# An attention backward kernel on one core: the scores S stay in the crossbar's key order in PSUM, and the exp reorders them

## The chip, the cores and the metric

The kernel runs on one core of a Trainium2 chip. The metric is the device time of one execution in microseconds; the time of a kernel is the median of several runs. A profile is one execution, taken by the hardware profiler.

In the text PE is TensorE (PEld its weight loads), DVE is VectorE, ACT is ScalarE, POOL is GpSimd and SP is SyncE, which here issues most of the transfers.

## The reference

Two independent attention blocks, A and B, each with 8 batches, 96 queries, model width 640, 32 heads of width 128 and a cache of 512 keys. The kernel computes the output and, for a given gradient of the output, the gradients of every input:

```
q      = (x @ wq) per head
scores = q @ k_cache^T * 128**-0.5          # 96 x 512 per batch and head
p      = softmax(scores)
o      = p @ v_cache
out    = (o of all heads) @ wo
outputs: out, and the gradients of x, k_cache, v_cache, wq, wo
```

So there are 2 x 32 x 8 = 512 pairs of a batch and a head. The text calls each of them a head.

## The kernel before

**Staging.** Heads are taken in pairs (HP = 2) with one batch at a time. A pair loads four tiles: K and V as they lie in memory (p_ldn, L256), and K and V transposed by the DMA crossbar (p_ldT, L242), each 256 KB for two heads. It stores two: dV and dK (p_st, L265). All six are issued by SP, in one queue and in the order of the program. KT_p, VT_p, K_sb and V_sb have four buffers each; dV_sb and dK_sb, the results on their way out, have two. GpSimd's queue issues the weights' loads and the other stores.

**Ticks.** Each head is cut into steps with a tick of their own (OFF): the scores at tick 3, P's transpose and dV at 4, the output at 5, dP and dS at 6, dS's transpose and dK at 7, dQ at 8. One tick takes one step of each of several heads. An Emitter sorts the steps by tick and by a slot within it; the scores, the exp and P are written with a higher priority, and the program's builder orders each engine's instructions from that. Between the heads' steps lie projections, weight gradients and the sums over heads (lines 215, 230, 440, 455, 477 and 512), which the text calls other matmuls.

**The steps of a head.**

- L285, PE: S = QT_h^T x KT into one PSUM bank of 96 x 512 f32.
- L287, DVE: the negated maximum of each row of S.
- L297, ACT: the exp of S, from PSUM to E_sb in bf16, with the row sums.
- L307, DVE: the reciprocal of the sums. L316, POOL: P_sb = E_sb times it.
- L339, PE: P_sb transposed; L345, ACT: copied out. L356, PE: dV; L361, ACT: copied out.
- L332, PE: the output of the head; L342, DVE: copied out. L370, POOL: its product with dO.
- L380, PE: dP = dOT_h^T x VT, also 96 x 512 f32. L382, PE: the row term dl.
- L384, DVE: dS = (dP - dl) * P.
- L406, PE: dS transposed; L408, DVE: copied out. L422, PE: dK; L427, ACT: copied out. L399, PE: dQ; L412, ACT: copied out.

**The order of the keys.** The crossbar's tile has for each of 128 partitions 64 x 16 elements: for each (f, c) 16 neighbouring values, 8 of one head and 8 of the other. Key number is r * 64 + f * 4 + c, with r from 0 to 7, f from 0 to 15 and c from 0 to 3. Everything behind the softmax wants the keys in the order (c, r, f), because K_sb and V_sb are cut into four chunks by c. For K the view is turned into that order when the matmul reads it, so that the innermost walk is over f, 64 elements (128 bytes) apart. For V the matmul reads (f, c, r), with runs of 8 neighbours, so dP lies in PSUM in that order, and L384 turns it with its read pattern: its innermost walk is over f, 32 f32 numbers (128 bytes) apart.

Of the kernel before, what the change touches and what calls it, by code (L numbers as in the profile page):

```python
# [7 lines left out]
ACT = mybir.ActivationFunctionType  # L8
# [48 lines left out]
def build_block(tc, em, tick0, blk, x, kc, vc, wq, wo, g_all, out_all, dx, dk, dv, dwq, dwo, ident, ones, pools, HG=4, first=True, groups=None):  # L57
    nc = tc.nc
# [7 lines left out]
    KC = Sk // 128  # L66
    scale = float(Dh) ** -0.5
# [35 lines left out]
    CS = pools["CS"]  # L103
# [131 lines left out]
    F4 = Sk // R8 // KC  # L235

    def p_ldT(h, b, which):
        def f():
            key = "KT" if which == 0 else "VT"
            t_ = kvp.tile([128, F4 * KC, 16], BF16, name=key + "_p", bufs=4)  # L240
            src = (kc if which == 0 else vc)[b, h:h + HP].rearrange("h (r f) d -> (h r) (f d)", r=R8)
            nc.sync.dma_start_transpose(t_[:], src)  # L242
            for j in range(HP):
                half = t_[:, :, j * R8:(j + 1) * R8]
                if which == 0:
                    CS.setdefault((blk, h + j, b), {})[key] = half.rearrange("p (f c) r -> p c r f", c=KC)
                else:
                    CS.setdefault((blk, h + j, b), {})[key] = half.rearrange("p (f c) r -> p f c r", c=KC)
        return f

    def p_ldn(h, b, which):
# [39 lines left out]
    def c_s2b(h, b):  # L291
        def f():
            with tc.high_priority(PRIO_OFF):
                st = CS[(blk, h, b)]
                E_sb = wk.tile([Sq, Sk], BF16, name="E_sb", bufs=2)
                rowsum = wk.tile([Sq, 1], F32, name="rowsum", bufs=3)
                nc.scalar.activation(E_sb[:], st["S_ps"][:], ACT.Exp, bias=st["negm"][:], scale=1.0, accum_out=rowsum[:])  # L297
                st["E_sb"], st["rowsum"] = E_sb, rowsum
                del st["S_ps"]
        return f  # L300
# [229 lines left out]
    for g in range(NG):  # L530
        h0 = GH0[g]
        for hh in range(groups[g]):
            h = h0 + hh
            j = h % HP
# [170 lines left out]
```

## Time and profile before

| | us |
|---|---|
| median of 3 runs | 2016.59 |
| lowest and highest run | 2014.18, 2019.17 |
| the profiled execution | 2013.47 |
| its span, first to last instruction | 2011.7 |
| DVE busy, ACT busy | 1439.6, 1359.0 |
| POOL busy | 723.5 |

The profile has a page with the shares of each engine, the transfer queues, the chain of work that ended last, and groups of instructions by line. Further views are the timeline, the waits, and a table of windows, with busy time for any stretch of the span. A row of a group gives line, engine, operation, output and input, shapes and count; behind the bar come busy time, the mean of one in ns, and the idle time ahead of it with what ended it. Matmuls overlap on PE, and a duration there holds the time from the first input to the last output, so that the distance between two starts is what an instruction costs the next one.

### The profile page before, as it was taken

Reading aid. Unit: us, or ns where it says so; the run is one execution under the profiler, and the core shown is the slowest. Engines: PE = TensorE matmul, PEld = TensorE weight load, DVE = VectorE, ACT = ScalarE, POOL = GpSimd, SP = SyncE. Lnnn points to the kernel's source line nnn. Section 1 sums busy time; section 2 is a strip of 40 time slices with the busy share of each in tenths; the row PEclk is TensorE's granted clock in tenths of the full one; section 3 lists DMA queues with packets and bytes.
Section 4 is the critical chain, followed back from the end, with each engine's and each line's share of the span. In section 5 each row is a group of like instructions: output and inputs, shape, how many; then the busy total and the mean of one; then the engine's idle time right before and its main releaser. Section 6 shows DMA issues by size and latency. Waiting matters only on the chain.

```text
span 2011.7 us, 59742 instructions
## 1 busy us (share of the span) xinstructions
PE 1957.6 (97%) x22648; PEld 1370.4 (68%) x22648; DVE 1439.6 (72%) x3597; ACT 1359.0 (68%) x3529; POOL 723.5 (36%) x1322
## 2 busy tenths in 40 slices
PE   6999999999999999998999999999999999999998
PEld 4667676676767667666666676767667676676766
DVE  4776777777777777777676767777777777777776
ACT  4877866767666676765666777666676766767663
POOL 3333333333333333334354333333333333333335
PEclk9999999999999999999999999999999999999999
DMA  8998989988889888888889989888898989979883
GB/s 246 257 263 214 251 233 232 251 223 240 228 223 244 230 243 223 235 234 227 213 247 266 253 226 249 226 236 234 232 240 220 238 231 237 252 211 239 229 217 127
DMA packets 322913, 468.88 MB, mean 233 GB/s; under 512 B 37472, under 2 KB 301152, under 8 KB 314432
## 3 DMA queue, kind: packets, MB, share of 16 engines
q1 hardware_dynamic: 304672, 404.75, 77.2%
q0 software_dynamic: 17952, 60.31, 9.1%
q8 instruction: 177, 2.90, 0.6%
q14 instruction: 112, 0.92, 0.1%
HBM read 171.57 MB, written 159.12 MB: 164 GB/s over the span
## 4 chain that ended last, share of the span: by engine, by line
PE 91%; DMA 3%; issue 2%; DVE 2%; POOL 1%; ACT 1%; POOLq 0%; SPq 0%; DVEq 0%; ACTq 0%
PE S_ps L285 21%; PE q_ps L215 10%; PE o_ps L512 9%; PE dV_ps L356 5%; PE dK_ps L422 5%; PE dP_ps L380 5%; PE dwq_ps L477 5%; PE dwo_ps L455 5%; PE dq_dst_ps L406 4%; PE optp_ps L339 4%; PE optp_ps L332 4%; PE dq_dst_ps L399 4%; PE n_ps L230 3%; PE nat_ps L440 2%; DMA out_dram<-ob 1%
## 5 line engine op out<-in xcount | busy, mean ns | idle before, releaser
L297 ACT ACTIVATE E_sb<-S_ps,negm 96x512 bf16<-96x512 f32 x512 | 348.2, 680 | 379.1 <-DVE negm L287 377.0
L287 DVE TENSOR_REDUCE negm<-S_ps 96x1 f32<-96x512 f32 x512 | 351.3, 686 | 257.8 <-PE S_ps L285 256.5
L285 PE MATMUL S_ps<-KT_p,QT_h 128*96 128x512 bf16 x512 | 521.8, 1019 | 2.6 <-DVE ob L523 1.2
L316 POOL TENSOR_SCALAR P_sb<-E_sb,rinv 96x512 bf16<-96x512 bf16 x512 | 352.4, 688 | 417.1 <-DVE rinv L307 414.1
L370 POOL TENSOR_TENSOR prod<-OT_h,dOT_h 128x96 bf16<-128x96 bf16 x512 | 186.7, 365 | 682.6 <-DVE OT_h L342 668.7
L384 DVE SCALAR_TENSOR_TENSOR dS_sb<-dP_ps,dl_ps,P_sb 96x512 bf16<-96x512 f32 x512 | 383.0, 748 | 50.7 <-PE dl_ps L382 37.6
L427 ACT ACTIVATE dK_sb<-dK_ps 128x512 bf16<-128x512 f32 x512 | 301.7, 589 | 159.1 <-PE dK_ps L422 111.2
L361 ACT ACTIVATE dV_sb<-dV_ps 128x512 bf16<-128x512 f32 x512 | 306.5, 599 | 4.4 <-PE dV_ps L356 3.2
L345 ACT ACTIVATE PT_sb<-optp_ps 128x384 bf16<-128x384 bf16 x512 | 251.2, 491 | 0.6 <-PE optp_ps L339 0.5
L356 PE MATMUL dV_ps<-dOnat_h,P_sb 96*128 96x128 bf16 x2048 | 199.6, 220 | 0.0
L422 PE MATMUL dK_ps<-Qnat_h,dS_sb 96*128 96x128 bf16 x2048 | 199.4, 220 | 0.0
L380 PE MATMUL dP_ps<-VT_p,dOT_h 128*96 128x512 bf16 x512 | 196.9, 385 | 0.0
L408 DVE COPY dST_sb<-dq_dst_ps 128x384 bf16<-128x384 bf16 x512 | 177.4, 346 | 23.7 <-PE dq_dst_ps L406 22.9
L406 PE MATMUL dq_dst_ps<-ident,dS_sb 96*128 96x96 bf16 x2048 | 173.2, 207 | 16.4 <-DVE dS_sb L384 16.4
L512 PEld LDWEIGHTS <-OT_h 128*128 128x128 bf16 x1152 | 101.4, 99 | 118.7 <-issue 104.1
L512 PEld LDWEIGHTS <-dQT_h 128*128 128x128 bf16 x1152 | 102.3, 99 | 115.9 <-issue 97.5
L339 PE MATMUL optp_ps<-ident,P_sb 96*128 96x96 bf16 x2048 | 172.8, 206 | 2.9 <-POOL P_sb L316 2.2
L332 PE MATMUL optp_ps<-PT_sb,V_sb 128*128 128x96 bf16 x2048 | 173.4, 207 | 0.0
L399 PE MATMUL dq_dst_ps<-dST_sb,K_sb 128*128 128x96 bf16 x2048 | 171.7, 207 | 0.0
L477 PEld LDWEIGHTS <-x_nat 128*128 128x128 bf16 x1920 | 120.8, 98 | 58.2 <-issue 46.6
L399 PEld LDWEIGHTS <-K_sb 128*128 128x128 bf16 x2048 | 134.2, 98 | 35.2 <-issue 16.7
L512 PE MATMUL o_ps<-wo_r,OT_h 128*128 128x256 bf16 (+1 forms) x1152 | 152.6, 256 | 0.2 <-ACT E_sb L297 0.2
(79 smaller groups left out, 3471.6 us busy)
## 6 DMA issues: line engine op xcount, KB each, us to landing
out_dram<-dV_sb SPq DMA_DIRECT2D x256, 256.0 KB, 3.7
out_dram<-dK_sb SPq DMA_DIRECT2D x256, 256.0 KB, 3.8
V_sb<-in_A_v_cache_dram SPq DMA_DIRECT2D x128, 256.0 KB, 3.9
K_sb<-in_A_k_cache_dram SPq DMA_DIRECT2D x128, 256.0 KB, 3.9
V_sb<-in_B_v_cache_dram SPq DMA_DIRECT2D x128, 256.0 KB, 3.8
K_sb<-in_B_k_cache_dram SPq DMA_DIRECT2D x128, 256.0 KB, 3.9
out_dram<-dwo_sb POOLq DMA_DIRECT2D x64, 160.0 KB, 3.8
out_dram<-dwq_sb POOLq DMA_DIRECT2D x32, 320.0 KB, 6.0
```

The lines of the kernel that those rows point to most:

```text
L285: nc.tensor.matmul(S_ps[:], hs["QT_h"][:, tok], st["KT"], start=True, stop=True)
L287: nc.vector.tensor_reduce(negm[:], S_ps[:], axis=AX.X, op=ALU.max, negate=True)
L297: nc.scalar.activation(E_sb[:], st["S_ps"][:], ACT.Exp, bias=st["negm"][:], scale=1.0, accum_out=rowsum[:])
L316: nc.gpsimd.tensor_scalar(P_sb[:], st["E_sb"][:], st["rinv"][:], 0.0, op0=ALU.mult, op1=ALU.add)
L356: nc.tensor.matmul(dV_ps[:, c * 128:(c + 1) * 128], P_sb[:, c * 128:(c + 1) * 128], hs["dOnat_h"][:, b * 128:(b + 1) * 128], start=True, s ...
L361: nc.scalar.activation(dV_p[:, j], dV_ps[:], ACT.Identity, scale=1.0)
L380: nc.tensor.matmul(dP_ps[:], hs["dOT_h"][:, tok], st["VT"], start=True, stop=True)
L384: nc.vector.scalar_tensor_tensor(dS_sb[:].rearrange("q (a f) -> q a f", f=F4), dP_ps[:].rearrange("q (f a) -> q a f", f=F4), dl_ps[:, 0:1] ...
L399: nc.tensor.matmul(dQT_ps, st["K_sb"][:, c, :], st["dST_sb"][:, c * Sq:(c + 1) * Sq], start=(c == 0), stop=(c == KC - 1))
L422: nc.tensor.matmul(dK_ps[:, c * 128:(c + 1) * 128], dS_sb[:, c * 128:(c + 1) * 128], hs["Qnat_h"][:, b * 128:(b + 1) * 128], start=True, s ...
L427: nc.scalar.activation(dK_p[:, j], dK_ps[:], ACT.Identity, scale=1.0)
L512: nc.tensor.matmul(o_ps[:], src[:, t * 128:(t + 1) * 128], rhs, start=(hh == 0), stop=(hh == groups[g] - 1))
```

## The change

The view of K is now the one of V, so S lies in PSUM in the order (f, c, r). The maximum does not depend on the order. The exp reads S with the pattern that L384 uses for dP, and writes E_sb contiguously in the order (c, r, f), as before.

```
@@ p_ldT
             for j in range(HP):
                 half = t_[:, :, j * R8:(j + 1) * R8]
-                if which == 0:
-                    CS.setdefault((blk, h + j, b), {})[key] = half.rearrange("p (f c) r -> p c r f", c=KC)
-                else:
-                    CS.setdefault((blk, h + j, b), {})[key] = half.rearrange("p (f c) r -> p f c r", c=KC)
+                CS.setdefault((blk, h + j, b), {})[key] = half.rearrange("p (f c) r -> p f c r", c=KC)
@@ c_s2b
-                nc.scalar.activation(E_sb[:], st["S_ps"][:], ACT.Exp, bias=st["negm"][:], scale=1.0, accum_out=rowsum[:])
+                nc.scalar.activation(E_sb[:].rearrange("q (a f) -> q a f", f=F4), st["S_ps"][:].rearrange("q (f a) -> q a f", f=F4), ACT.Exp, bias=st["negm"][:], scale=1.0, accum_out=rowsum[:])
```

F4 is 16, and a stands for the 32 values of (c, r).

## The prediction

> **What bounds the kernel now.** I read the page first: shares, queues, chain, groups.
>
> ```profile
> PE 1957.6 (97%) x22648; PEld 1370.4 (68%) x22648; DVE 1439.6 (72%) x3597; ACT 1359.0 (68%) x3529; POOL 723.5 (36%) x1322
> ...
> DMA packets 322913, 468.88 MB, mean 233 GB/s; under 512 B 37472, under 2 KB 301152, under 8 KB 314432
> ...
> q1 hardware_dynamic: 304672, 404.75, 77.2%
> q0 software_dynamic: 17952, 60.31, 9.1%
> q8 instruction: 177, 2.90, 0.6%
> q14 instruction: 112, 0.92, 0.1%
> ...
> PE 91%; DMA 3%; issue 2%; DVE 2%; POOL 1%; ACT 1%; POOLq 0%; SPq 0%; DVEq 0%; ACTq 0%
> ...
> L297 ACT ACTIVATE E_sb<-S_ps,negm 96x512 bf16<-96x512 f32 x512 | 348.2, 680 | 379.1 <-DVE negm L287 377.0
> L287 DVE TENSOR_REDUCE negm<-S_ps 96x1 f32<-96x512 f32 x512 | 351.3, 686 | 257.8 <-PE S_ps L285 256.5
> L285 PE MATMUL S_ps<-KT_p,QT_h 128*96 128x512 bf16 x512 | 521.8, 1019 | 2.6 <-DVE ob L523 1.2
> ...
> L384 DVE SCALAR_TENSOR_TENSOR dS_sb<-dP_ps,dl_ps,P_sb 96x512 bf16<-96x512 f32 x512 | 383.0, 748 | 50.7 <-PE dl_ps L382 37.6
> ```
>
> PE is busy for 97% of the span of 2011.7 us (the span's own row stands with the windows below) and 91% of the chain, so TensorE is the bound. The costliest thing on it is the S matmul, 512 times 1019 ns. Two other numbers matter later. DVE and ACT are busy about 70% each, off the path. And the DMA rows add up to 77.2 + 9.1 + 0.6 + 0.1 = 87.0% of the sixteen engines' span, or 0.870 x 2011.7 = 1750 us of transfer time. That is more than DVE's, and it is hidden only because PE takes longer.
>
> Next the timeline of one ordinary head (the columns are start, duration, engine, line): TensorE's rows in order, and the one of VectorE that belongs to them.
>
> ```profile
> 1002.17 0.38 PE L380 MATMUL dP_ps<-VT_p,dOT_h 128*96 128x512 bf16 x1
> 1002.39 0.16 PE L382 MATMUL dl_ps<-ones,prod 128*96 128x1 bf16 x1
> 1002.42 0.38 PE L455 MATMUL dwo_ps<-g_nat,Onat 128*128 128x512 bf16 x1
> 1002.63 1.02 PE L285 MATMUL S_ps<-KT_p,QT_h 128*96 128x512 bf16 x1
> 1003.47 1.26 PE L455 MATMUL dwo_ps<-g_nat,Onat 128*128 128x512 bf16 x5
> 1004.57 0.33 PE L399 MATMUL dq_dst_ps<-dST_sb,K_sb 128*128 128x96 bf16 x4
> 1004.74 0.34 PE L406 MATMUL dq_dst_ps<-ident,dS_sb 96*128 96x96 bf16 x4
> ...
> 1002.62 0.75 DVE L384 SCALAR_TENSOR_TENSOR dS_sb<-dP_ps,dl_ps,P_sb 96x512 bf16<-96x512 f32 x1 [0.22 <-PE dl_ps L382]
> ```
>
> The matmul dP has the same shape as S, 128 x 512 with 96 rows out, from a tile that the same transposing load fills. It differs in the order in which it walks that tile. PE starts the instruction behind S after 1003.47 - 1002.63 = 0.84 us, and the one behind dP after 1002.39 - 1002.17 = 0.22 us. Durations overlap on PE, so the distance between starts is the price.
>
> **The change, part by part.** *The S matmul* walks KT_p as dP walks VT_p, in runs of 8 neighbouring elements instead of single elements 128 bytes apart. It should cost what dP costs: 0.84 - 0.22 = 0.62 us less, 512 times, 317 us. All of it lies on PE, the bound. (By the durations it would be 1019 - 380, or 327 us; I take the starts.) From the profiled execution's 2013.47 us, which is its span of 2011.7 and 1.8 around it, this leaves 1696 us if nothing else comes late.
>
> *The maximum* (L287) reads the same 512 numbers of the bank contiguously in another order: nothing.
>
> *The exp* (L297) now reads PSUM with 128 bytes between neighbours and still writes E_sb contiguously. No ACT row shows such a read. The nearest row is L384 on DVE, which reads dP_ps in just this pattern at 748 ns. L287, a contiguous read of the same 96x512 f32, takes 686. So the stride costs at most 62 ns there, though L384 does more besides. From below, nothing suggests a gain, so 0. From above stands what the stride cost PE: 0.62 us. I take the middle of the DVE row, 30 ns, 16 us of ACT time in all, because L384 reads the same memory by the same pattern. ACT then has 1359 + 16 = 1375 us of work, and even with 0.62 us it would have 1359 + 317 = 1676, under the 1696 of PE. On the path it costs nothing while that cover lasts.
>
> The Trainium skill speaks against this part: "PSUM — Partial Sum Buffer", section Specifications (TRN2), gives PSUM lines of 8 bytes and says that a non-contiguous pattern slows matmuls a good deal. Here no matmul has one in PSUM, ACT has; by a penalty of PE's size the sum would still be that of PE. The L384 row speaks against so large a penalty.
>
> No instruction, wait or transfer is added or moved.
>
> *What is late next, among the engines.* PE per head falls from 2011.7 / 512 = 3.93 to 3.31 us; DVE has 1439.6 / 512 = 2.81 and ACT 2.69, so neither is the bound on average. The handoffs tighten. dS ends at 1002.62 + 0.75 = 1003.37, and PE wants it at 1004.74: of 1.37 us of slack 0.75 stays, since one S lies between. It is tighter in a head without other matmuls:
>
> ```profile
> 1965.83 1.02 PE L285 MATMUL S_ps<-KT_p,QT_h 128*96 128x512 bf16 x1
> 1966.67 0.35 PE L399 MATMUL dq_dst_ps<-dST_sb,K_sb 128*128 128x96 bf16 x4
> 1966.90 0.34 PE L406 MATMUL dq_dst_ps<-ident,dS_sb 96*128 96x96 bf16 x4
> ...
> 1969.25 0.35 PE L399 MATMUL dq_dst_ps<-dST_sb,K_sb 128*128 128x96 bf16 x4
> ...
> 1966.09 0.75 DVE L384 SCALAR_TENSOR_TENSOR dS_sb<-dP_ps,dl_ps,P_sb 96x512 bf16<-96x512 f32 x1 [0.27 <-PE dl_ps L382]
> ```
>
> There dS ends at 1966.84, 0.06 us ahead of its use, so such a head loses 0.56 of its 0.62 us again. An estimate: with 3.93 us for a mean head against 1969.25 - 1966.67 = 2.58 for this one (its L399 group to the next one's), most heads have over a microsecond of other matmuls between; I put one head in eight at this loss, 64 x 0.56 = 36 us. So PE alone would give 1696 + 36 = 1732 us.
>
> *What is late next, among the transfers.* The windows view shows how full the DMA engines can be (the last two columns are their busy share and GB/s):
>
> ```profile
> core 0 of [0], span 2011.7 us
> core 0: us, PE busy (x) PEld busy (x) DVE busy (x) ACT busy (x) POOL busy (x), PEclk, DMA share, GB/s
> 0.00:50.00 50.00, 34.70 (x333) 23.19 (x334) 23.12 (x53) 22.04 (x49) 16.57 (x31) 0.97 0.86 246
> 50.00:100.00 50.00, 47.30 (x541) 30.77 (x539) 37.37 (x90) 40.14 (x105) 18.71 (x35) 1.00 1.00 260
> 480.00:520.00 40.00, 39.93 (x473) 27.78 (x471) 30.93 (x79) 29.24 (x78) 15.06 (x29) 1.00 0.99 266
> 1950.00:2011.00 61.00, 52.37 (x650) 40.13 (x647) 40.64 (x105) 27.60 (x72) 33.29 (x62) 0.97 0.47 146
> ```
>
> Where the share is 0.99 to 1.00 the rate is 260 to 266 GB/s. At 1732 us the kernel would ask for 468.88 MB / 1732 us = 271 GB/s on average, its slow start and end included. So the transfers become the bound. First way: 1750 us of transfer time, and the ends, where the engines cannot be full. They idle 0.14 x 50 = 7 us in the first window and 0.53 x 61 = 32 us in the last. 1750 + 39 = 1789. Second way, by bytes: the two ends carry 246 x 50 = 12.3 MB and 146 x 61 = 8.9 MB; the remaining 447.7 MB at 266 GB/s take 1683 us, at 260 GB/s 1722; with the ends' 111 us, shorter by 0.62 us for each of the heads in them (an estimate: six in each, since about half of either window goes to heads of 3.93 us), that is 1683 + 111 - 7 = 1787, or 1826.
>
> **The transfers would come earlier by themselves**, because the queue that issues them waits for PE:
>
> ```profile
> SPq L256 <- PE dK_ps L422: 371.5, 205, 3.4
> ```
>
> These are waits for a buffer that PE is still reading. When PE frees it sooner, the load starts sooner. The one transfer with little room is the store: dV_sb and dK_sb have two buffers, so a store must land within the two heads of the next pair. Where the share was highest, in the window from 50, the chain already ran through it:
>
> ```profile
> 89.04 3.85 DMA out_dram<-dK_sb
> ```
>
> So I expect the loss to show as ACT waiting at L361 and L427 for stores, and PE behind it.
>
> I forecast 1789 us for the span and 1.8 around it: **1790 us**, 224 less than the profiled execution. That one is 0.15% under the median of 2016.59, well inside the range here.
>
> **The rivals.** *The transfers are elastic and PE stays the bound.* The busy share counts the time that packets took, and packets that share an engine or wait for memory count too long; then 1750 us is no floor. The result would be 1732 us, or 1698 if the handoffs cost nothing. For it: no PE wait of weight names a load in steady state, though the share was 0.99 from 480 to 520 with PE busy 39.93 of 40. Against it: the two full windows stop at 260 and 266 GB/s. The Trainium skill is on this side: "DMA: Bandwidth & Descriptors", section Where 436 GB/s comes from, puts the ceiling at 435 GB/s, which would make an estimated 468.88 / 435, or 1078 us. No window here comes near it.
>
> *The stores' landing stops the pair loop before the engines are full.* In the window from 50, PE was busy 47.30 of 50. If that share of its own 1696 + 36 us were all it could hold throughout, the time would be 1732 x 50 / 47.30 = 1831, and where the DMA engines also only reach 0.95, 1750 / 0.95 + 39 = 1881.
>
> *Slower: the exp.* If a 128-byte stride in PSUM costs ACT the ratio that the stride in KT_p costs PE, 0.84 / 0.22 = 3.8, the exp takes 680 x 3.8 = 2584 ns, 1904 more. ACT would have 1359 + 975 = 2334 us and be the bound: 2336 us. This decides from (2011.7 - 1359.0) / 512 = 1.27 us more for each exp on. For it: no ACT row excludes it. Against it: L384.
>
> *No effect.* The matmul's 1.02 us could come from something other than the order of KT_p. Then 2013 us stays. dP's 0.38 us from the same kind of tile speaks against it strongly.
>
> **How the numbers follow.** Transfers bound, 1750 to 1850: 0.55, and this is the forecast. PE bound, 1698 to 1750: 0.29. The stores' loop, 1831 to 1900: 0.10. Slower by the exp: 0.03. No effect: 0.03. The range goes from 1700 to 1860: it holds the first two cases and half of the third, and leaves out about 0.15 with the tails. A run of this kernel can tell 0.3%, 6 us, from no change. Faster by more than that is 0.94, the same 0.03, slower 0.03.
>
> **What would show it.** L285 at about 385 ns; L297 between 680 and 745; L287 and L384 unchanged; the four DMA rows adding to 96 to 100% of the new span, with 260 GB/s or more on average; PE below 95% with idle time; L361 and L427 waiting for out_dram for tens of microseconds. The forecast is wrong in its mechanism if the DMA share stays near 0.9 while PE is still over 95% busy, or if the transfer time itself shrinks well below 1750 us; in its first step, if L285 stays over 500 ns; and in its cover, if L297 rises over 1 us.

## The result and the profile after

The changed kernel takes 1817.21 us, the median of three runs (1807.46 to 1818.08), against 2016.59. The ratio is 0.900, with a 95% interval from 0.895 to 0.905. The forecast was 1790, so the gain is 199 us where 227 were forecast from the same median. The profiled execution took 1818.08 us. Each engine has its instructions in the same order in both kernels; the line numbers behind L245 are smaller by three.

The page of the changed kernel, with the rows that answer to those of before:

```profile
span 1816.3 us, 59529 instructions
...
PE 1662.7 (92%) x22474; PEld 1381.8 (76%) x22648; DVE 1396.9 (77%) x3597; ACT 1352.2 (74%) x3529; POOL 723.8 (40%) x1322
...
DMA packets 322912, 468.87 MB, mean 258 GB/s; under 512 B 37472, under 2 KB 301152, under 8 KB 314432
...
q1 hardware_dynamic: 304672, 404.75, 86.1%
q0 software_dynamic: 17952, 60.31, 10.2%
q8 instruction: 177, 2.90, 0.7%
q14 instruction: 111, 0.91, 0.1%
...
L294 ACT ACTIVATE E_sb<-S_ps,negm 96x512 bf16<-96x512 f32 x512 | 348.9, 681 | 213.4 <-DVE negm L284 205.6
...
L381 DVE SCALAR_TENSOR_TENSOR dS_sb<-dP_ps,dl_ps,P_sb 96x512 bf16<-96x512 f32 x512 | 382.1, 746 | 43.7 <-PE dl_ps L379 33.5
...
L282 PE MATMUL S_ps<-KT_p,QT_h 128*96 128x512 bf16 x512 | 198.2, 387 | 3.3 <-ACT dK_sb L424 0.8 <-ACT E_sb L294 0.8 <-DVE ob L520 0.7
```

S fell from 1019 to 387 ns, and the exp takes 681 where it took 680. PE is busy for 92% instead of 97%, and the four transfer rows add up to 97.1%, or 1764 us of 1816.3. That is the picture that the prediction drew; only the mean rate, 258 GB/s, stays a little under the 260 that it asked for. The new idle time on PE shows in the view of the waits (total, times, longest):

```profile
ACT dK_sb L424 <- DMA out_dram<-dK_sb: 56.1, 45, 3.3
...
ACT dV_sb L358 <- DMA out_dram<-dV_sb: 27.0, 20, 4.0
...
PE dq_dst_ps L403 <- DVE dS_sb L381: 24.5, 24, 1.6
PE o_ps L509 <- ACT dK_sb L424: 24.2, 17, 2.8
...
PE dq_dst_ps L396 <- ACT dV_sb L358: 17.2, 12, 3.9
```

ScalarE waits 83 us for stores of dK and dV, where it waited 2 us before, and PE waits behind it. The timeline of one such stall, the rows of SP's queue (SPq) and those of ACT and PE that belong to it:

```profile
671.19 0.58 ACT L424 ACTIVATE dK_sb<-dK_ps 128x512 bf16<-128x512 f32 x1
...
672.74 3.63 SPq L242 DMA_TRANSPOSE KT_p<-in_A_k_cache_dram  x1
...
675.52 0.60 ACT L358 ACTIVATE dV_sb<-dV_ps 128x512 bf16<-128x512 f32 x1
...
677.09 0.42 SPq L262 DMA_DIRECT2D out_dram<-dK_sb  x1
...
678.76 0.60 ACT L358 ACTIVATE dV_sb<-dV_ps 128x512 bf16<-128x512 f32 x1 [1.44 <-DMA out_dram<-dV_sb]
...
679.37 3.76 SPq L242 DMA_TRANSPOSE KT_p<-in_A_k_cache_dram  x1
...
682.70 0.60 ACT L424 ACTIVATE dK_sb<-dK_ps 128x512 bf16<-128x512 f32 x1 [2.81 <-DMA out_dram<-dK_sb]
...
683.22 0.53 SPq L262 DMA_DIRECT2D out_dram<-dV_sb  x1
683.35 0.60 PE L509 MATMUL o_ps<-wo_r,OT_h 128*128 128x128 bf16 x6 [2.42 <-ACT dK_sb L424]
```

A tile holds two heads, and its store can leave when the copy of the second one has ended. The dK tile whose second copy starts at 671.19 is complete by 671.77. Its store leaves at 677.09, because SP is busy from 672.74 with the issue of one transposing load, for 3.63 us, and with a load behind it. Two pairs later, dK's copy needs this buffer again: it waits 2.81 us, until the store has landed, and starts at 682.70, and PE stands still for 2.42 us. The dV tile completed at 676.12 fares no better: its store leaves at 683.22, behind another such issue of 3.76 us. So stores are late twice: they stand in SP's queue, and then they take long to land. Over the whole trace, a store of dK leaves 3.4 us after its tile is complete (the median; 2.2 for dV), where it was 0.3 and 0.2 before, and SP spends 84% of the span on issues instead of 60%. The view of line 242 says that for K's transposing load the long issues are the rule now (ns, lowest/median/highest); before:

```profile
L242 SPq DMA_TRANSPOSE KT_p<-in_A_k_cache_dram x128: 1095/1144/7989, 1.8 to 964.1; - x128
```

and after:

```profile
L242 SPq DMA_TRANSPOSE KT_p<-in_A_k_cache_dram x128: 1095/2346/7577, 1.8 to 870.9; - x128
```

V's transposing load keeps its short issue, a median of 1164 ns.

Two theories fit all this. By the prediction's (T), the transfers need some 1750 us whatever else happens, and the late stores are how that floor is felt. By the other, the transfers have room, and it is the stores' path alone, SP's queue (Q) or the two buffers (L), that stops the loop.

### The profile page after: what moved, and what is told of

It is laid out like the page before. It is cut to its first block, busy times and chain, and to the rows that moved or that the text cites. A ratio compares the mean times of both kernels' runs of the same rounds, so it can differ in the third digit from the quotient of the medians.

```text
span 1816.3 us, 59529 instructions
## 1 busy us (share of the span) xinstructions
PE 1662.7 (92%) x22474; PEld 1381.8 (76%) x22648; DVE 1396.9 (77%) x3597; ACT 1352.2 (74%) x3529; POOL 723.8 (40%) x1322
## 5 line engine op out<-in xcount | busy, mean ns | idle before, releaser
L424 ACT ACTIVATE dK_sb<-dK_ps 128x512 bf16<-128x512 f32 x512 | 302.4, 591 | 142.5 <-PE dK_ps L419 70.2
L284 DVE TENSOR_REDUCE negm<-S_ps 96x1 f32<-96x512 f32 x512 | 347.5, 679 | 53.3 <-PE S_ps L282 52.0
L358 ACT ACTIVATE dV_sb<-dV_ps 128x512 bf16<-128x512 f32 x512 | 307.2, 600 | 33.3 <-DMA out_dram<-dV_sb 27.0
L282 PE MATMUL S_ps<-KT_p,QT_h 128*96 128x512 bf16 x512 | 198.2, 387 | 3.3 <-ACT dK_sb L424 0.8
L403 PE MATMUL dq_dst_ps<-ident,dS_sb 96*128 96x96 bf16 x2048 | 175.4, 208 | 24.9 <-DVE dS_sb L381 24.5
L509 PE MATMUL o_ps<-wo_r,OT_h 128*128 128x256 bf16 (+1 forms) x1152 | 156.5, 261 | 21.6 <-ACT dK_sb L424 21.6
L304 DVE RECIPROCAL rinv<-rowsum 96x1 f32<-96x1 f32 x512 | 80.0, 156 | 124.2 <-ACT E_sb L294 103.3
L509 PE MATMUL o_ps<-wqT_h,dQT_h 128*128 128x256 bf16 (+1 forms) x1152 | 151.0, 256 | 6.3 <-ACT E_sb L294 3.6
L339 DVE CAST OT_h<-optp_ps 128x96 bf16<-128x96 f32 x512 | 126.9, 248 | 32.6 <-PE optp_ps L336 29.0
```

What stands on the lines that cost most here:

```text
L284: nc.vector.tensor_reduce(negm[:], S_ps[:], axis=AX.X, op=ALU.max, negate=True)
L358: nc.scalar.activation(dV_p[:, j], dV_ps[:], ACT.Identity, scale=1.0)
L424: nc.scalar.activation(dK_p[:, j], dK_ps[:], ACT.Identity, scale=1.0)
L509: nc.tensor.matmul(o_ps[:], src[:, t * 128:(t + 1) * 128], rhs, start=(hh == 0), stop=(hh == groups[g] - 1))
```

## The experiments

**The engines without the stream.**

```
 p_ldT, p_ldn: t_ = one of the first four tiles, for the fifth pair and all behind it
 p_st:         only for h == 0 and b < 2
```

> The changed kernel without its stream of keys and values: of the K and V tiles only the first four of each kind are loaded and then used again for every pair, and dV and dK are stored for two pairs only. All computing instructions stay. It measures the floor of the engines and their handoffs. Theory T (the transfers bound the changed kernel): 1700 to 1750 us, the 1732 of the prediction. Rival H (handoffs between the engines bound it, the full transfer queues only go with that): 1790 us or more, close to the 1817 of the changed kernel.

It took 1704.18 us:

```profile
span 1702.4 us, 56168 instructions
...
PE 1635.8 (96%) x22648; PEld 1356.5 (80%) x22648; DVE 1391.7 (82%) x3597; ACT 1343.5 (79%) x3529; POOL 723.6 (43%) x1322
```

So the engines and their handoffs alone give 1704 us, and the stream of keys and values costs the changed kernel 113 us. (This run, like the transfers alone, both halved stores, the missing transposing loads and the exp's part, is a single execution. Executions of one kernel lie up to 26 us apart here, and medians of the kernel before differ by up to 7 us from chip to chip.) By the spans, some 87 us of that is idle time of PE (1816.3 - 1662.7 = 153.6 against 1702.4 - 1635.8 = 66.6; in the changed kernel's trace 174 matmul records are missing, so its idle time is a little less) and 27 us or more is busy time: the matmuls of dV and dK took 222 ns each in the changed kernel and 219 here, at a mean granted clock of 0.976 and 0.997. The handoff from dS to L403 (L421 in this kernel) cost PE 25.7 us here, about as much as in the changed kernel (24.5).

**The transfers without the engines.**

```
 Emitter.run keeps only the steps that start transfers;
 p_st, qB, qD and gU store constant tiles
```

> The transfers of the changed kernel alone: the same loads, transposing loads and stores with their sizes, queues and order; nothing is computed, and all stores read constant tiles, so that no transfer waits for an engine. Theory T: 1650 to 1790 us, as the prediction's 1750 us of transfer time is a floor. Rival E (the transfer time is elastic, packets count too long when engines share the memory): under 1550 us, at 300 GB/s or more.

It took 1543.55 us:

```profile
span 1541.8 us, 1913 instructions
...
DMA  9999999999999999999999999999999999999999
GB/s 321 329 320 330 329 328 329 341 328 346 347 284 288 295 288 290 294 286 290 286 296 286 289 297 296 289 277 296 295 290 297 286 297 280 280 300 289 295 288 298
...
q1 hardware_dynamic: 304672, 404.75, 91.7%
q0 software_dynamic: 17952, 60.31, 11.0%
```

This takes theory T's ground away. The same transfers need no more than 1542 us when nothing else runs, with a mean of 302 GB/s, and their shares add up to 102.7%, so the rows of the queues can sum to over 100%. SP's queue spends 95% of this span on issues, so that even these 1542 us may be the time of one queue and not a limit of the transfer engines. They moved 320 to 347 GB/s while GpSimd's queue took part, and about 290 when SP's queue was alone. The 1750 us of before were no floor.

**A third buffer for the results.**

```
-st["dV_p"] = wk.tile([128, HP, KC * 128], BF16, name="dV_sb", bufs=2)
+st["dV_p"] = wk.tile([128, HP, KC * 128], BF16, name="dV_sb", bufs=3)
 (dK_sb likewise; the staging pool stp from 3 buffers to 2)
```

> The changed kernel with three buffers instead of two for dV_sb and for dK_sb, and one less for a staging tile of block B's start to make room. ScalarE's waits for stores (56 + 27 us in the changed kernel) should nearly go. Theory T: the transfers still need their time, 1780 to 1815 us. Rival L (only the landing of a store against two buffers holds the loop, the transfers have room): 1730 to 1750 us.

It took 1765.79 us, a ratio of 0.876 (0.873 to 0.879) to the kernel before. That lies between what the two theories expected. ScalarE's waits for stores fell to about half, not to nothing:

```profile
ACT dK_sb L424 <- DMA out_dram<-dK_sb: 29.9, 21, 3.0
...
ACT dV_sb L358 <- DMA out_dram<-dV_sb: 13.5, 11, 2.2
```

Not one byte less is moved, and 50 us are gone, so T fails a second time. But SP's queue is no quicker (KT_p's issue has a median of 2356 ns). A store of dK now leaves 8.4 us after its tile is complete (the median; 7.1 for dV), so lateness takes up the new buffer too.

**The stores on another queue.**

```
-            nc.sync.dma_start(dst.rearrange("h (p c) d -> p h (c d)", c=KC), t_[:])
+            nc.gpsimd.dma_start(dst.rearrange("h (p c) d -> p h (c d)", c=KC), t_[:])
```

> The changed kernel with the stores of dV and dK issued by GpSimd's queue instead of SP's, so that no store stands behind a load that waits for its buffer or behind the issue of a transposing load. Theory T: no great change, 1790 to 1830 us. Rival Q (SP's single queue, where an issue of a transposing load takes 1.3 to 2.5 us, makes the stores late): 1730 to 1760 us.

It took 1752.52 us, a ratio of 0.870 (0.867 to 0.872). That is what rival Q expected. A store now leaves 0.3 to 0.4 us after its tile is complete, and the waits for stores fall from 83 to 24 us:

```profile
ACT dK_sb L424 <- DMA out_dram<-dK_sb: 22.6, 16, 2.4
...
PE optp_ps L336 <- POOL P_sb L313: 28.3, 46, 1.4
```

The second row is the price: GpSimd also makes P_sb, and PE now waits 28.3 us for it instead of 8.4. The edit changes a second thing: GpSimd's queue moves the stores' 134 MB in 40960 packets, SP's in 139264. The next run keeps the packets as they were.

**The stores on ScalarE's queue.** The same edit with nc.scalar in place of nc.gpsimd.

> The changed kernel with the stores of dV and dK issued by ScalarE's queue, right behind its own copy, in the hardware's descriptors as on SP. If a queue of their own is what the stores need (theory Q): 1740 to 1765 us, like the stores on GpSimd's queue (1752.5); the builder also orders some of the engines' instructions anew. If ScalarE pays for the issues (512 times about 0.5 us, as they take on SP): 1790 us or more.

It took 1775.97 us, a ratio of 0.877 (0.872 to 0.882), between the two expectations. ScalarE's waits for stores fall to 14.7 us, and yet PE waits 48.5 us for ScalarE, summed over all its lines, against 68.4 in the changed kernel and 15.8 with GpSimd's queue. The packets are the 139264 of before, so a queue of their own helps the stores without larger packets; this one costs part of it again. Whether the packets have a part in the 23 us between the two queues was not separated.

**Both cures at once**, three buffers and GpSimd's queue.

> The changed kernel with the stores on GpSimd's queue and three buffers for dV_sb and dK_sb. ScalarE's remaining waits for stores (22.6 us for dK_sb with the queue alone) should go. Theory: what is left above the engines' 1704 us is mostly those waits and P_sb coming late from GpSimd (28 us at L336): 1725 to 1745 us. Rival: the two cures are the same one, 1750 us.

It took 1748.62 us, a ratio of 0.865 (0.863 to 0.868). The expectation of 1725 to 1745 missed, and the rival held: the cures overlap. No wait of ScalarE for a store of dV or dK is left; PE waits 31.5 us for P_sb.

**Both, with only dV's stores on GpSimd's queue** and dK's on SP's.

> The changed kernel with three buffers for dV_sb and dK_sb, the dV stores on GpSimd's queue and the dK stores left on SP's. If SP's queue with all six transfers of a pair is what falls behind, and GpSimd with all the stores delays P_sb, half of each should be best: 1725 to 1745 us. If what is left is the general crowding of the transfer engines, it gives nothing over all stores on GpSimd: 1745 to 1760 us.

It took 1750.43 us, a ratio of 0.869 (0.865 to 0.872). Sharing the stores out gives nothing over putting them all on GpSimd. K's transposing load in block A takes 2843 ns to issue here, longer than in the changed kernel, and yet ScalarE waits only 10.4 us for stores: a long issue costs little where what stands behind it has room.

**Half of the stored bytes.**

```
-dma_start(dst.rearrange("h (p c) d -> p h (c d)", c=KC), t_[:])
+dma_start(dst.rearrange("h (p c) d -> p h (c d)", c=KC)[:, 0:1], t_[:, 0:1])
```

> The changed kernel with half of each dV and dK store left out: only the first head of a pair is stored, 128 KB instead of 256, from the same queue, with the same number of issues. This takes 67 of 469 MB away and leaves SP's queue its order. Theory C (SP's queue falls behind because the transfer engines are nearly full, and an issue of a transposing load then takes 2.5 us): the issue of KT_p falls to 1.7 us or less, the stores leave within 1 us and the time is 1715 to 1745 us. Rival Q (the order in the queue alone, stores behind loads that wait for their buffers, makes them late): 1780 us or more.

It took 1737.06 us, with the queue's order untouched. KT_p's issue:

```profile
L242 SPq DMA_TRANSPOSE KT_p<-in_A_k_cache_dram x128: 1098/1822/8016, 1.8 to 824.7; - x128
...
L242 SPq DMA_TRANSPOSE KT_p<-in_B_k_cache_dram x128: 1095/1674/9778, 831.4 to 1677.0; - x128
```

The time is as theory C expected, and the issue falls from 2346 to some 1750 ns, a little less far than it said. The stores leave 0.9 us after their half tile is complete, by the median; theory C had all of them within 1 us. ScalarE waits 5.3 us for stores. So the order of SP's queue alone does little harm; it does when the transfers around it are many.

The same edit on the kernel before:

> The kernel before with half of each dV and dK store left out, as in the run of the changed kernel with halved stores. If TensorE bounds the kernel before and its transfers are hidden: 2000 to 2015 us, no change by over 1%. If the transfers cost it time too: 1950 us or less.

It took 2013.27 us, against a median of 2016.25 for the kernel before on the same chip. There TensorE hides the transfers.

**The same bytes less, as transposing loads.**

```
-em.add(ct + OFF["vt"], SLOTS["LOAD"], p_ldT(h, b, 1))
-nc.tensor.matmul(dP_ps[:], hs["dOT_h"][:, tok], st["VT"], start=True, stop=True)
+nc.tensor.matmul(dP_ps[:], hs["dOT_h"][:, tok], st["KT"], start=True, stop=True)
```

> The changed kernel without the transposing loads of V; dP is computed from KT instead, so that its values are others. This takes away 67 MB, as many as the halved stores did (1737 us), but as transposes. If bytes alone count: 1730 to 1745 us. If the transposing loads are the dear ones, because SP's queue stands still while they are issued: 1705 to 1725 us, the engines' floor.

It took 1717.31 us, 13 us above the engines alone and 20 below the halved stores:

```profile
q1 hardware_dynamic: 292384, 337.61, 71.5%
...
L242 SPq DMA_TRANSPOSE KT_p<-in_A_k_cache_dram x128: 1101/1109/7788, 1.8 to 831.8; - x128
```

With one transposing load per pair its issue takes 1109 ns throughout. The queue q1 carries the same 338 MB as with halved stores, in 0.715 x 1715.5 = 1227 us against 0.786 x 1735.3 = 1364 us. This points to a transposed byte being dearer than a stored one, but it rests on shares, which swell when transfers crowd, and on 20 us between two single executions. What the traces show firmly is that the changed kernel's long issues of KT_p are gone when V's transposing load is (with as many bytes less, the halved stores left some 1750 ns), though SP still has to wait for buffers: its queue issues for only 46% of the span, and the waits lie between the issues.

**The exp's part alone**, on the kernel before.

> The kernel before with the exp's new read pattern alone, S still being written in key order, so that the exp's output stands in a wrong order. It prices the strided PSUM read on ScalarE: if it is free, 2005 to 2020 us and 681 ns for the exp; by the dS row 710 ns and no change of time either; if the stride costs as on PE, 1300 ns and, with that cover, 2020 to 2100 us.

It took 2018.19 us, and the exp 680 ns:

```profile
L297 ACT ACTIVATE E_sb<-S_ps,negm 96x512 bf16<-96x512 f32 x512 | 348.3, 680 | 381.1 <-DVE negm L287 378.6
```

This strided read of PSUM is free on ScalarE.

## Why the prediction was right, and where it was not

**The S matmul** was right: 387 ns where dP takes 388, and dP took 380 by the timeline of before. In the changed kernel PE starts the instruction behind S after 0.21 to 0.22 us (between 500 and 520 us), as it does behind dP.

**The exp** was right in that nothing hangs on it; the 30 ns per exp were 1. The Trainium skill's rule on lines of 8 bytes in PSUM ("PSUM — Partial Sum Buffer", Specifications (TRN2)) is given there for matmuls, and it does not carry over to ScalarE's read here: 680 and 681 ns at a step of 128 bytes. The rival "Slower: the exp" put the price of PE's stride, 3.8 times, on this read and is out too.

**The handoffs** were put at 36 us above 1696; the engines alone took 1704, so they cost some 8; PE's idle time rose by 12.5, from 54.1 to 66.6. They come at the same few places as before (16.4 us at L406 before, 25.7 without the stream), and the heads without other matmuls were fewer than one in eight, or lose less than the working had.

**The transfers as a floor** is the step that failed. The prediction took 87.0% of the span, 1750 us, for work that has to be done in any case, and a full share for the limit. Alone, the same transfers took 1542 us. The prediction's own sign of a wrong mechanism, a transfer time well below 1750 us, does not show in the changed kernel (1764 us); it took the run without engines to see it. The share measures how long packets are under way, and it counts more when they crowd each other: the sum was 1764 us at 258 GB/s in the changed kernel and 1583 us (1.027 x 1541.8) at 302 GB/s alone. The reading "the two full windows stop at 260 and 266 GB/s" took for a ceiling what was none: alone, the transfers moved 320 to 347 GB/s in their first slices and about 290 after them. The rival that doubted it, "the transfers are elastic and PE stays the bound", was right about the share. It was wrong about the time, 1732 us at most, since PE does not stay the bound alone.

**Where the loss shows** was right: ScalarE waits at L358 and L424 for the stores, and PE behind it. The prediction took these waits for the way in which a floor is felt and gave the stores' loop a tenth of its own. The runs turn that round. Of the 113 us between the engines' 1704 and 1817, about 50 go with one more buffer, and about 60 with GpSimd's queue for the stores or 45 with ScalarE's (ratios of 0.876, 0.870 and 0.877 against 0.900; 0.001 is 2 us), all without a byte less. That the forecast of 1790 came near 1817 was partly luck: a floor that was too high stood in for a loop that was left out of the likeliest case.

**What stays open**: the last 45 us, from 1704 to the best version's 1749. Most of them go when V's transposing loads are taken out (1717), and some when stores are halved (1737), so the crowd of transfers is in them; PE's waits for P_sb (31.5 us, against 9.1 without the stream) are in them too in that version. How much of the rest is the lower granted clock (0.987 in that run, 0.997 without the stream), and how much is late data, was not separated. Why the issue of K's transposing load becomes long is open too: the runs show that it does with V's transposing load and many other transfers around it, not what holds it.

## What to carry to other kernels

When the bounding engine gets faster, sum the transfers against the new span, but price them by a run of the transfers alone, not by the busy share of a run that had room for them. Before that limit is reached, look at the queue: which small transfer with few buffers stands behind which slow issue, and who waits for its landing. A store path with its own queue, or one more buffer, was worth 45 to 60 us here, and both together little more.

## What the runs showed of the hardware

- A matmul's moving operand read in single bf16 elements 128 bytes apart cost 0.84 us per 512 columns between starts, in runs of 8 neighbours 0.22. The same step of 128 bytes in f32 on PSUM cost ScalarE nothing (681 against 680 ns).
- Transfer shares above 100%: 102.7% at 302 GB/s. The highest rate in a slice was 347 GB/s, with two queues at work. The Trainium skill's 435 GB/s ("DMA: Bandwidth & Descriptors", Where 436 GB/s comes from), from which the prediction worked out 1078 us, is the ceiling of the fabric there; for transfers between HBM and SBUF the same section has the HBM side bind, at about 358 GB/s. No run here reached either, but the 266 GB/s that the prediction held against it was no limit.
- The issue of K's transposing load on SP took 1.11 us when it was the only one of its pair, and 2.35 us behind V's at the changed kernel's pace, up to 3.76 in the stall shown; at the pace of before, behind V's as well, it took 1.14. While it lasts, everything behind it in the queue stands still.
